# Attention, routing and two MLPs on one core: probabilities times v in one go, and both heads' tails returned to partitions 0 to 63

## The chip, the cores and the metric

One NeuronCore of a Trainium2 chip runs the whole program. The metric is the device time of one execution in microseconds (us), lower being better. The kernel before took 1168.46 us as the median of three runs (1166.98 to 1168.68).

## The reference, cut to what matters

```
# q, k, v: (4, 12, 448, 64) float32; g_q, g_k: (64,)
rmsnorm(x, g) = x / sqrt(mean(x*x, -1) + 1e-6) * g
scores = 1/8 * rmsnorm(q, g_q) @ rmsnorm(k, g_k).T      # per batch and head, 448 x 448
attn   = exp(scores - rowmax) ; attn /= sum(attn) + 1e-9
x      = (attn @ v) gathered to 1792 tokens x 768
logits = x @ w_gate + modality_bias[modality_id]          # 8 experts
e      = argmax(logits); gate = softmax(logits)[e]
y      = gate * (relu(x @ w1[e]) @ w2[e])                 # each token by its one expert
out    = g(y @ w_in) @ w_out                              # g: 0, (h+1)^2/4 or h by range
```

## The kernel before, in words

The program has an attention stage (to about 346 us of the profile), then the experts, then a dense MLP. Attention works on 24 pairs of heads (six pairs per batch element). A pair has seven row tiles of scores: a head has 448 rows, three full tiles of 128 for each head (tiles 0 to 2 and 4 to 6), and one tile (3) for the 64 last rows, the tail, of both heads together.

The loop of lines 453 to 466 walks over slots n = 7p + u, with p the pair and u the tile. In a slot TensorE transposes the probabilities of five slots ago (`turn_p`, L284) and makes the scores of this slot (`scores`, L264). ScalarE takes the exponentials (`expo`, L275). VectorE and ScalarE share the copies of the transposed probabilities (`take_p`, L304 and L306). VectorE takes the row maxima (`row_max`, L269). All else hangs on the table `sched`, filled by `put(z + off, f, p)` with z = 7p: functions in a slot are issued in the order in which they were put, and each engine takes its instructions in that order. Below, "slot z+9" means nine slots after the pair's first. The table `place` gives some early pairs other slots.

What touches the change:

- `mix` (L308) multiplies probabilities and v into the tile `av`, one PSUM bank with one buffer: parts 0 and 1 in slot z+11, parts 2 and 3 in slot z+13. L316 has 128 rows of the array and 64 columns (one head), L320 has 64 by 64 (the tail). `mixed` (L325) copies `av` to SBUF on ScalarE in slot z+13.
- `back` (L334), slot z+15, turns the result back by a matmul with `comb`, which holds an identity and the router's weights: three matmuls for full rows (L341), two of 64 by 64 for the tails (L343), which leave one head's tail on partitions 0 to 63 and the other's on 64 to 127, all in one tile `xo`.
- `invert` (L327), slot z+13: the reciprocal of the sums; an addition (L330, GpSimd from the fourth pair on) and a reciprocal on VectorE (L332).
- `finish_pair` (L1536), slot z+15: three VectorE operations scale `xo` into `x`, `lg` and `xt` (L1542, L1544, L1545). After a batch element's last pair it also sends `x` and `xt` to DRAM and calls `bias_into`.
- `Route.columns` (L603) is a generator that the loop advances one step at a time by `tick`: a step that yields `True` ahead of a TensorE step waits for the next slot with u = 0. Its first TensorE step is the fold (L619), which brings the second head's tail logits to the lower partitions.
- In PSUM the tag `tq` has two buffers. A pair's slots use it in this order: `xo` (z+15), and for the pairs ahead `turn_k` part 0, `turn_q` part 1, `turn_k` part 1, `turn_q` part 0. For a pair p+2, `turn_k` part 0 (L234), `k_low` part 0 (L241, VectorE, the reader that frees it) and `turn_k` part 1 fall in slots z+9, z+10 and z+11 of pair p. In slot z+11 the table holds `mix` parts 0 and 1 ahead of that `turn_k` part 1.
- For pair p+3, `q_low` (L208, GpSimd) is put in slot z+9 of pair p, after the functions of pair p, and `turn_q` part 0 (L217) in slot z+12.

After the loop the last pair's rest is written out by hand (lines 469 to 475), and `on_route` (L1209) advances the routing between the experts' matmuls; `SKIP` names the points at which it makes no TensorE step.

Of the kernel before, what the change touches and what calls it, by code (L numbers as in the profile page):

```python
# [16 lines left out]
E = 8  # L17
# [6 lines left out]
WARM = 40  # L24
TICKS = 2
NPAIRS = 24
SKIP = (3, 4, 7)
KT = SLOTS // 128
NT = E * KT

# [1 line left out]
def attention(tc, ctx, q, k, v, const, ps, late, finish_pair, tick, early):  # L32
# [7 lines left out]
    nc = tc.nc  # L40
    B, H, S, D = q.shape
# [285 lines left out]
    def invert(p):  # L327
        R = st[p]
        d = sm_p.tile([128, 7], F32, name="d", tag="d", bufs=3)
        (nc.vector if p < 3 else nc.gpsimd).tensor_scalar(out=d, in0=R["sum"], scalar1=1.0, scalar2=1e-9, op0=ALU.mult, op1=ALU.add)  # L330
        R["r"] = sm_p.tile([128, 7], F32, name="r", tag="r", bufs=3)
        nc.vector.reciprocal(out=R["r"], in_=d)  # L332

    def back(p):  # L334

        R = st[p]
        r = p % (H // 2)
        t = ps.tile([128, 7, 72], F32, name="xo", tag="tq")
        o = R["o"]
        for c in range(3):  # L340
            nc.tensor.matmul(out=t[:, 2 * c:2 * c + 2], lhsT=o[:, 128 * c:128 * c + 128], rhs=comb[:, r], start=True, stop=True)  # L341
        for i, h in enumerate(halves2):
            nc.tensor.matmul(out=t[h, 6], lhsT=o[h, 384:S], rhs=comb[h, r, i], start=True, stop=True)  # L343
        R["xo"] = t

    def finish(p):
        R = st[p]
        finish_pair(*divmod(p, H // 2), R["xo"], R["r"])
        st[p] = None


# [12 lines left out]
    def put(n, f, p, *a):  # L364
        m = place.get(p, {}).get(f.__name__, n)
        sched.setdefault(m if type(m) is int else m[a[0]], []).append((f, (p,) + a))
# [12 lines left out]
            put(z + off, f, bt[0])  # L379
    for p in range(NP):  # L380
        z = 7 * p
        put(z + 11, mix, p, (0, 1))
        put(z + 13, mix, p, (2, 3))
        for off, f in ((-16, scale_k), (-15, scale_q), (-13, q_high), (-12, q_low), (13, invert), (13, mixed), (15, back), (15, finish)):
# [93 lines left out]
class Route:  # L478
# [7 lines left out]
    def __init__(self, tc, const, cp, tmp, ps, ps_tag, ident):  # L486
        nc = tc.nc
        self.nc, self.tc, self.ps, self.ps_tag = nc, tc, ps, ps_tag
        self.cp, self.tmp, self.ident = cp, tmp, ident
        C = lambda shape, name, dt=F32: cp.tile(shape, dt, name=name)  # L490

        def iota(t, pattern, base, mult):
            nc.gpsimd.iota(t, pattern=pattern, base=base, channel_multiplier=mult, allow_small_or_imprecise_dtypes=True)
            return t
        self.cold = iota(C([128, NDEST], "cold"), [[1, NDEST]], 0, 0)
        self.pcol = iota(C([128, 1], "pcol"), [[0, 1]], 0, 1)
        self.d14 = iota(C([128, E], "d14"), [[-KT, E]], 0, 1)
# [8 lines left out]
        self.fold = C([128, 64], "fold")  # L506
# [12 lines left out]
        self.lg = C([128, 16, E], "lgs")  # L519
        nc.gpsimd.memset(self.lg, 0.0)  # L520
        self.tok, self.gat = C([128, 128], "tok", F32R)[0:NT], C([128, 128], "gat")[0:NT]
        self.base = C([128, 5, E], "base")
        self.gate = C([128, 16], "gate")
        self.midx = const.tile([128, NDEST], I32, name="midx")
        self.pidx = const.tile([128, NDEST], I32, name="pidx")
        self.gslot = const.tile([128, NDEST], F32, name="gslot")
        self.first = const.tile([1, 1], I32, name="first")
        self.ctl = const.tile([1, 2, NDEST], I32, name="ctl")

    def copies(self):  # L530
# [3 lines left out]
        for p in (slice(0, 64), slice(64, 128)):  # L534
            nc.scalar.activation(out=self.fold[p], in_=self.ident[p, p], func=ACTF.Copy)

    def load(self, modality_id, modality_bias):
        nc, mid = self.nc, self.mid
# [56 lines left out]
    def bias_into(self, dst, b):  # L595

        nc = self.nc
        nc.vector.memset(dst, 0.0)
        bm = self.bm[:, 4 * b:4 * b + 4]
        nc.vector.tensor_copy(out=dst[:, 0:6].rearrange("p (c i) e -> p c i e", i=2)[:, :, 0], in_=bm[:, 0:3])  # L600
        nc.vector.tensor_copy(out=dst[0:64, 6], in_=bm[0:64, 3])

    def columns(self, b, parts):  # L603

# [10 lines left out]
        ls = T([128, 7, E], "ls")  # L615
# [6 lines left out]
        lv = ls[:, 0:6].rearrange("p (c i) e -> p c i e", i=2)  # L622
        tt(out=lb[:, 0:3], in0=lv[:, :, 0], in1=lv[:, :, 1], op=ALU.add)
# [852 lines left out]
def tile_kernel(ctx: ExitStack, tc: tile.TileContext, q, k, v, g_q, g_k, moe_modality_id, moe_w_gate, moe_modality_bias,  # L1476
                moe_w1, moe_w2, moe2_w_in, moe2_w_out, out):
    nc = tc.nc
    with tc.manual_schedule():
# [8 lines left out]
        with ExitStack() as c0:  # L1488
# [44 lines left out]
            X = {}  # L1533
            steps, last_wait = [], [0]

            def finish_pair(b, r, xo, rc):  # L1536
                if r == 0:
                    X[b] = (xp.tile([128, 3, 12, 64], F32, name="x", tag="x"), xp.tile([128, 6, 64], F32, name="xt", tag="xt"),
                            rt.tile([128, 7, 7, E], F32, name="lg", tag="lg"))
                x, xt, lg = X[b]  # L1540
                rb = rc.rearrange("p (u o) -> p u o", o=1)
                nc.vector.tensor_tensor(out=x[:, :, 2 * r:2 * r + 2], in0=xo[:, 0:6, 0:64].rearrange("p (c i) d -> p c i d", i=2),  # L1542
                                        in1=rb[:, 0:6].rearrange("p (c i) o -> p c i o", i=2).to_broadcast([128, 3, 2, 64]), op=ALU.mult)
                nc.vector.tensor_tensor(out=lg[:, :, r], in0=xo[:, :, 64:72], in1=rb.to_broadcast([128, 7, E]), op=ALU.mult)  # L1544
                nc.vector.tensor_scalar(out=xt[:, r], in0=xo[:, 6, 0:64], scalar1=rc[:, 6:7], scalar2=None, op0=ALU.mult)  # L1545
                if r == 5:
                    t0 = 448 * b
                    nc.sync.dma_start(out=xt_d[t0:t0 + 384].rearrange("(p c) d -> p c d", c=3), in_=x.rearrange("p c h d -> p c (h d)"))
                    tv = xt_d[t0 + 384:t0 + 448].rearrange("p (r i d) -> p i r d", i=2, d=64)
                    for i in range(2):  # L1550
                        nc.sync.dma_start(out=tv[:, i], in_=xt[64 * i:64 * i + 64])
                    route.bias_into(lg[:, :, 6], b)
                    steps.append([route.columns(b, lg), False])

            moe.m.ps, moe.m.turn_tag = ps, "tq"
# [52 lines left out]
```

## Time and profile before

| | |
|---|---|
| median of the runs | 1168.46 us |
| profiled execution | 1169.01 us, its span 1167.3 us |
| TensorE (PE) busy | 1135.8 us, 97% of the span |
| VectorE (DVE) busy | 826.2 us, 71% |
| ScalarE (ACT) busy | 677.4 us, 58% |
| GpSimd (POOL) busy | 369.2 us, 32% |
| mean granted TensorE clock | 0.989 |

The profile's times are from the start of the span. Matmuls are pipelined: the printed durations overlap, so the cost of a group is read from its start to the start of the next. A float32 matmul shows as two records. "Idle before, releaser" is how long an engine stood still ahead of an instruction and what ended that. The profiled execution took 0.55 us longer than the median.

### The profile page before, as it was taken

The page shows a single profiled execution, that of the slowest core. Times are in us where ns is not written, and L with a number is a line of the kernel's source. Part 1 is how long each engine was busy: PE and PEld are TensorE (multiplying, and loading weights), DVE is VectorE, ACT ScalarE, POOL GpSimd, SP SyncE. Part 2 cuts the span into 40 slices and gives each one's busy share as a digit, 9 for nine tenths or more (in the row PEclk, how much of TensorE's full clock was granted, in tenths as well). Part 3 has the DMA queues.
Part 4 walks back from the last instruction along what each step waited for, and adds up shares of the span by engine and source line. Part 5 has one row for each costly group of instructions (what it writes and reads, how often), then busy time and mean ns, then how long its engine had stood idle before and what let it go on. Part 6 is the DMA issues. An engine that isn't in the chain of part 4 may idle for free. (4 is left out here: it accounts for less than half of the span.)

```text
span 1167.3 us, 20022 instructions
## 1 busy us (share of the span) xinstructions
PE 1135.8 (97%) x7093; PEld 957.5 (82%) x7093; DVE 826.2 (71%) x1551; ACT 677.4 (58%) x1374; POOL 369.2 (32%) x571
## 2 busy tenths in 40 slices
PE   6999999999999999999999999999999999999997
PEld 5667777777768998999999978888888888888996
DVE  6776877877757667888989978884644446444674
ACT  5778777777643566665555645544534345433664
POOL 4666565645220203255544434440200010000100
PEclk8999999999998999999999999999999999999999
DMA  4323324322227689899999723340200001000100
GB/s 105 80 72 87 112 64 117 82 57 80 59 67 245 194 285 295 276 324 289 286 291 310 250 88 99 106 132 4 109 1 1 1 28 55 1 1 1 56 1 28
DMA packets 144593, 138.17 MB, mean 118 GB/s; under 512 B 39134, under 2 KB 125150, under 8 KB 143972
## 3 DMA queue, kind: packets, MB, share of 16 engines
q1 hardware_dynamic: 139822, 120.04, 33.8%
q0 software_dynamic: 4000, 16.53, 4.0%
q8 instruction: 58, 0.95, 0.3%
q14 instruction: 51, 0.42, 0.1%
q10 hardware_dynamic: 662, 0.23, 0.1%
HBM read 117.23 MB, written 18.10 MB: 116 GB/s over the span
## 5 line engine op out<-in xcount | busy, mean ns | idle before, releaser
L934 DVE TENSOR_TENSOR l<-ld,h 128x768 fp32r<-128x768 f32 x159 | 151.5, 970 | 18.4 <-ACT h L929 15.5
L906 POOL TENSOR_SCALAR cva<-cva 128x384 f32<-128x384 f32 x64 | 110.2, 1724 | 144.0 <-ACT cva L905 143.8
L929 ACT ACTIVATE h<-ld 128x768 fp32r<-128x768 f32 x159 | 130.5, 840 | 10.1 <-PE hs L953 6.5
L1426 POOL DMA_INDIRECT out_dram<-ld,oidx x11 | 13.0, 1182 | 336.1 <-ACT ld L1423 212.4
L275 ACT ACTIVATE P<-s,nb 128x448 f32<-128x448 f32 x144 | 91.3, 634 | 34.1 <-DVE nb L269 29.9
L269 DVE TENSOR_REDUCE nb<-s 128x1 f32<-128x448 f32 x168 | 102.6, 614 | 10.7 <-PE s L264 10.1
L1378 ACT ACTIVATE u<-hp,half 128x512 f32<-128x512 f32 (+1 forms) x64 | 40.4, 631 | 108.5 <-PE hp L942 108.5
L1385 DVE SCALAR_TENSOR_TENSOR w<-u 128x512 f32<-128x512 f32 (+1 forms) x64 | 39.9, 623 | 85.3 <-ACT u L1378 85.2
L306 DVE COPY pT<-pt 128x448 f32<-128x448 f32 x96 | 59.6, 621 | 55.6 <-PE pt L284 55.4
L942 PE MATMUL hp<-yh,h 128*128 128x512 f32 (+1 forms) x384 | 89.0, 368 | 2.3 <-PEq L1329 2.3
L976 PE MATMUL a<-l,gh 128*128 128x512 f32 x240 | 89.8, 403 | 0.0
L976 PE MATMUL a<-h,gh 128*128 128x512 f32 x240 | 89.0, 400 | 0.0
L976 PE MATMUL a<-h,gl 128*128 128x512 f32 x240 | 88.8, 399 | 0.0
L1150 ACT ACTIVATE rh<-hp 128x256 fp32r<-128x256 f32 x64 | 24.6, 384 | 109.2 <-PE hp L942 106.8
L942 PE MATMUL hp<-yl,h 128*128 128x512 f32 (+1 forms) x384 | 87.5, 364 | 0.0
L942 PE MATMUL hp<-yh,l 128*128 128x512 f32 (+1 forms) x384 | 87.2, 363 | 0.0
L1393 DVE TENSOR_TENSOR gl<-u,gh 128x512 fp32r<-128x512 f32 (+1 forms) x64 | 40.3, 629 | 64.2 <-ACT gh L1392 64.1
L284 PE MATMUL pt<-ident,P 128*128 128x128 f32 x504 | 83.9, 275 | 0.1
L1392 ACT ACTIVATE gh<-u 128x512 fp32r<-128x512 f32 (+1 forms) x64 | 36.9, 576 | 81.2 <-PE a L977 78.6
L942 PEld LDWEIGHTS hp<-yl,h 128*128 128x128 f32 x384 | 67.1, 190 | 11.4
L942 PEld LDWEIGHTS hp<-yh,h 128*128 128x128 f32 x384 | 64.6, 191 | 14.0 <-PEq L1329 2.6
L942 PEld LDWEIGHTS hp<-yh,l 128*128 128x128 f32 x384 | 66.7, 189 | 11.2
(331 smaller groups left out, 3200.9 us busy)
## 6 DMA issues: line engine op xcount, KB each, us to landing
ld<-in_moe_w_dram SPq DMA_DIRECT2D x160, 384.0 KB
raw<-in_moe_w_in_dram SPq DMA_DIRECT2D x32, 384.0 KB
ld<-in_moe_w_out_dram SPq DMA_DIRECT2D x26, 384.0 KB
rawk<-in_k_dram SPq DMA_DIRECT2D x24, 192.0 KB
rawv<-in_v_dram SPq DMA_DIRECT2D x24, 192.0 KB
xt_d<-x SPq DMA_DIRECT2D x4, 1152.0 KB
kn<-kn SPq DMA_DIRECT2D x20, 224.0 KB
rawq<-in_q_dram SPq DMA_DIRECT2D x23, 192.0 KB
```

The source lines that it names most:

```text
L269: nc.vector.tensor_reduce(out=R["nb"][:, u:u + 1], in_=R["s", u], op=ALU.max, axis=AX.X, negate=True)
L275: nc.scalar.activation(out=o, in_=R.pop(("s", u)), func=ACTF.Exp, bias=R["nb"][:, u:u + 1], accum_out=R["sum"][:, w:w + 1])
L284: nc.tensor.transpose(out=out, in_=src, identity=ident)
L306: nc.vector.tensor_copy(out=R["PT", m], in_=t)
L906: nc.gpsimd.tensor_scalar(out=R["a"], in0=R["a"], scalar1=2.0 ** -15, scalar2=122879.9921875, op0=ALU.max, op1=ALU.min)
L929: nc.scalar.activation(out=h, in_=src, func=ACTF.Copy)
L934: (engine or self.nc.vector).tensor_tensor(out=l, in0=src, in1=h.bitcast(F32), op=ALU.subtract)
L942: nc.tensor.matmul(out=t[:, 0:n], lhsT=w[:, k], rhs=x[:, k, 0:n], start=i == 0 and k == 0, stop=i == 2 and k == 5)
L976: nc.tensor.matmul(out=a[j], lhsT=p[:, c], rhs=q[:, 0:512], start=first and i == 0, stop=last and i == 2)
L1378: nc.scalar.activation(out=u, in_=t[:, s], func=ACTF.Relu, scale=0.5, bias=half)
L1385: nc.vector.scalar_tensor_tensor(out=w, in0=u, scalar=1.0, in1=u, op0=ALU.min, op1=ALU.mult)
L1393: nc.vector.tensor_tensor(out=gl[:, 0:n], in0=u, in1=gh[:, 0:n].bitcast(F32), op=ALU.subtract)
```

## The change

- `mix` of a pair runs whole in slot z+13.
- `back` makes one matmul for both tails, with 64 output partitions and 144 columns, into a tile `xs` that shares the one buffer of `av`; `xo` keeps the full rows alone.
- `invert` moves to slot z+9 and issues a DMA from the GpSimd queue: the tail sums of the second head, 64 values on partitions 64 to 127, to partitions 0 to 63 (tile `rt`).
- `finish_pair` makes six VectorE operations: `x`, `lg` of full rows, and `xt` and `lg` for each head's tail. The tails' logits lie side by side, so `lg` has eight columns of tiles and the fold with its matmul, its PSUM tile and its two set-up copies on ScalarE goes; the second head's part is added by VectorE. `bias_into` (now two memsets and two copies) runs after the fifth pair of a batch element and not after the sixth. `xt` goes to DRAM by one DMA and not two.
- `SKIP` gets the point 0.

```
-SKIP = (3, 4, 7)
+SKIP = (0, 3, 4, 7)
...
     def invert(p):
...
         nc.vector.reciprocal(out=R["r"], in_=d)
+        R["rt"] = sm_p.tile([64, 1], F32, name="rt", tag="rt", bufs=3)
+        nc.gpsimd.dma_start(out=R["rt"], in_=R["r"][64:128, 6:7])
...
     def back(p):
...
-        for i, h in enumerate(halves2):
-            nc.tensor.matmul(out=t[h, 6], lhsT=o[h, 384:S], rhs=comb[h, r, i], start=True, stop=True)
-        R["xo"] = t
+        t2 = ps.tile([64, 2, 72], F32, name="xs", tag="av", bufs=1)
+        nc.tensor.matmul(out=t2, lhsT=R["o"][:, 384:S], rhs=comb[:, r], start=True, stop=True)
+        R["xo"] = t[:, 0:432].rearrange("p (u d) -> p u d", u=6), t2
...
-        put(z + 11, mix, p, (0, 1))
-        put(z + 13, mix, p, (2, 3))
-        for off, f in (..., (13, invert), (13, mixed), (15, back), (15, finish)):
+        put(z + 13, mix, p, (0, 1, 2, 3))
+        for off, f in (..., (9, invert), (13, mixed), (15, back), (15, finish)):
...
     def bias_into(self, dst, b):
-        nc.vector.memset(dst, 0.0)
+        nc.vector.memset(dst[:, :, 6], 0.0)
+        nc.vector.memset(dst[64:128, 6:8, 0:6], 0.0)
...
     def columns(self, b, parts):
...
         nc.vector.tensor_reduce(out=ls, in_=parts.rearrange("p u r e -> p u e r"), op=ALU.add, axis=AX.X)
-        yield True
-        pf = self.ps.tile([64, E], F32, name="pf", tag=self.ps_tag)
-        nc.tensor.matmul(out=pf, lhsT=self.fold, rhs=ls[:, 6], start=True, stop=True)
         yield False
...
-        nc.vector.tensor_copy(out=lb[0:64, 3], in_=pf)
+        tt(out=lb[0:64, 3], in0=ls[0:64, 6], in1=ls[0:64, 7], op=ALU.add)
...
-            def finish_pair(b, r, xo, rc):
+            def finish_pair(b, r, xo, xs, rc, rt_):
...
+                if r == 4:
+                    route.bias_into(lg, b)
...
-                nc.vector.tensor_tensor(out=lg[:, :, r], in0=xo[:, :, 64:72], in1=rb.to_broadcast([128, 7, E]), op=ALU.mult)
-                nc.vector.tensor_scalar(out=xt[:, r], in0=xo[:, 6, 0:64], scalar1=rc[:, 6:7], scalar2=None, op0=ALU.mult)
+                nc.vector.tensor_tensor(out=lg[:, 0:6, r], in0=xo[:, :, 64:72], in1=rb[:, 0:6].to_broadcast([128, 6, E]), op=ALU.mult)
+                for i, s in enumerate((rc[0:64, 6:7], rt_)):
+                    nc.vector.tensor_scalar(out=xt[:, r, i], in0=xs[:, i, 0:64], scalar1=s, scalar2=None, op0=ALU.mult)
+                    nc.vector.tensor_scalar(out=lg[0:64, 6 + i, r], in0=xs[:, i, 64:72], scalar1=s, scalar2=None, op0=ALU.mult)
```

## Rows read from the trace of the kernel before

**Rows 1.** Busy time by engine of two stretches: each engine's busy us, then clock, DMA share, GB/s

```profile
60.00:336.00 276.00, 272.51 (x1855) 196.26 (x1855) 211.05 (x533) 203.93 (x548) 148.28 (x330) 0.99 0.30 84
336.00:362.00 26.00, 21.32 (x134) 16.31 (x133) 16.69 (x62) 8.98 (x16) 3.38 (x4) 0.87 0.42 130
```

**Rows 2.** Timeline of PE in one pair: start, us, instruction, records, idle before

```profile
212.12 0.37 PE L264 MATMUL s<-kl,Q 128*128 128x448 f32 x1
212.42 1.72 PE L316 MATMUL av<-pT,rawv 128*64 128x448 f32 x8
214.07 0.55 PE L234 MATMUL tk<-ident,kn 128*128 128x128 f32 x3
...
216.56 0.97 PE L316 MATMUL av<-pT,rawv 128*64 128x448 f32 x4
217.47 0.98 PE L320 MATMUL av<-pT,rawv 64*64 64x384 f32 x6
218.37 0.33 PE L284 MATMUL pt<-ident,pm 128*128 128x128 f32 x1
...
220.56 0.37 PE L264 MATMUL s<-kl,Q 128*128 128x448 f32 x1
220.76 0.90 PE L341 MATMUL xo<-comb,osb 128*128 128x144 f32 x6
221.59 0.34 PE L343 MATMUL xo<-comb,osb 64*64 64x72 f32 x4
221.86 0.33 PE L284 MATMUL pt<-ident,pm 128*128 128x128 f32 x1
```

**Rows 3.** Timeline of PE around a fold

```profile
206.03 0.37 PE L264 MATMUL s<-kl,Q 128*128 128x448 f32 x1
206.33 0.28 PE L619 MATMUL pf<-ls,fold 128*64 128x8 f32 x2
206.54 0.44 PE L284 MATMUL pt<-ident,pm 128*128 128x128 f32 x2
```

**Rows 4.** Timeline of the start, DVE and PE

```profile
27.06 0.74 DVE L241 SCALAR_TENSOR_TENSOR kl<-tk,gg,kh 128x512 fp32r<-128x512 f32 x1
27.86 0.55 PE L234 MATMUL tk<-ident,kn 128*128 128x128 f32 x3 [0.63 <-DVE kl L241]
```

**Rows 5.** Timeline of DVE in a pair with no routing step, and PE's `mix` beside it

```profile
248.68 0.56 DVE L1542 TENSOR_TENSOR x<-xo,r 128x384 f32<-128x384 f32 x1 [0.39 <-PE xo L343]
249.16 0.20 DVE L1544 TENSOR_TENSOR lg<-xo,r 128x56 f32<-128x56 f32 x1
249.28 0.28 DVE L1545 TENSOR_SCALAR xt<-xo,r 128x64 f32<-128x64 f32 x1
249.47 0.61 DVE L306 COPY pT<-pt 128x448 f32<-128x448 f32 x1
...
251.36 0.62 DVE L269 TENSOR_REDUCE nb<-s 128x1 f32<-128x448 f32 x1 [0.74 <-PE s L264]
251.90 0.74 DVE L241 SCALAR_TENSOR_TENSOR kl<-tk,gg,kh 128x512 fp32r<-128x512 f32 x1
252.33 0.60 PE L316 MATMUL av<-pT,rawv 128*64 128x448 f32 x2
```

**Rows 6.** Timeline of DVE and PE in a pair with routing steps

```profile
146.62 0.60 PE L316 MATMUL av<-pT,rawv 128*64 128x448 f32 x2
146.84 0.74 DVE L241 SCALAR_TENSOR_TENSOR kl<-tk,gg,kh 128x512 fp32r<-128x512 f32 x1
```

**Rows 7.** The operations on tile `lg`: count, ns min/median/max

```profile
L601 DVE COPY lg<-bm x4: 678/679/2200, 117.2 to 347.5; 64x8 f32<-64x8 f32 x4
```

**Rows 8.** Timeline of POOL and PE in slot z+10 of the fourth pair

```profile
77.25 1.13 POOL L208 TENSOR_TENSOR qs<-qn,qs 128x448 fp32r<-128x448 f32 x1 [1.76 <-ACT qs L203]
...
78.44 0.54 PE L217 MATMUL tq<-identr,qs 128*128 128x128 f32 x4 [2.11 <-DVE yi L124]
```

**Rows 9.** Timeline of POOL: a DMA that it issues

```profile
370.24 1.04 POOL L1049 DMA_INDIRECT xg<-xt_d,midx  x1 [0.31 <-issue]
```

**Rows 10.** Timeline of PE at the end of attention

```profile
347.49 0.63 PE L987 MATMUL tp<-ident,xg 128*128 128x128 f32 x4 [1.06 <-DVE lg L598]
...
353.54 0.26 PE L669 MATMUL pr<-oh,tri_r 128*128 128x40 f32 x1 [1.92 <-DVE oh L641]
```

More of the change, by code (lines that the diff above doesn't have):

```diff
@@ L337, in back @@
         r = p % (H // 2)
-        t = ps.tile([128, 7, 72], F32, name="xo", tag="tq")
-        o = R["o"]
+        t = ps.tile([128, 512], F32, name="xo", tag="tq")
         for c in range(3):
-            nc.tensor.matmul(out=t[:, 2 * c:2 * c + 2], lhsT=o[:, 128 * c:128 * c + 128], rhs=comb[:, r], start=True, stop=True)
-        for i, h in enumerate(halves2):
-            nc.tensor.matmul(out=t[h, 6], lhsT=o[h, 384:S], rhs=comb[h, r, i], start=True, stop=True)
-        R["xo"] = t
+            nc.tensor.matmul(out=t[:, 144 * c:144 * c + 144], lhsT=R["o"][:, 128 * c:128 * c + 128], rhs=comb[:, r], start=True, stop=True)
+        t2 = ps.tile([64, 2, 72], F32, name="xs", tag="av", bufs=1)
+        nc.tensor.matmul(out=t2, lhsT=R["o"][:, 384:S], rhs=comb[:, r], start=True, stop=True)
+        R["xo"] = t[:, 0:432].rearrange("p (u d) -> p u d", u=6), t2
     def finish(p):
         R = st[p]
-        finish_pair(*divmod(p, H // 2), R["xo"], R["r"])
+        finish_pair(*divmod(p, H // 2), *R["xo"], R["r"], R["rt"])
         st[p] = None
@@ L381, in attention @@
         z = 7 * p
-        put(z + 11, mix, p, (0, 1))
-        put(z + 13, mix, p, (2, 3))
-        for off, f in ((-16, scale_k), (-15, scale_q), (-13, q_high), (-12, q_low), (13, invert), (13, mixed), (15, back), (15, finish)):
+        put(z + 13, mix, p, (0, 1, 2, 3))
+        for off, f in ((-16, scale_k), (-15, scale_q), (-13, q_high), (-12, q_low), (9, invert), (13, mixed), (15, back), (15, finish)):
             put(z + off, f, p)
@@ L505, in __init__ @@
         self.tri_r, self.ones_r = C([128, 128], "tri_r", F32R), C([128, 128], "ones_r", F32R)
-        self.fold = C([128, 64], "fold")
         self.bias = C([128, 2, E], "bias")
@@ L533, in copies @@
         nc.scalar.activation(out=self.ones_r, in_=self.ones, func=ACTF.Copy)
-        for p in (slice(0, 64), slice(64, 128)):
-            nc.scalar.activation(out=self.fold[p], in_=self.ident[p, p], func=ACTF.Copy)
     def load(self, modality_id, modality_bias):
@@ L597, in bias_into @@
         nc = self.nc
-        nc.vector.memset(dst, 0.0)
+        nc.vector.memset(dst[:, :, 6], 0.0)
+        nc.vector.memset(dst[64:128, 6:8, 0:6], 0.0)
+        v = dst[:, :, 6].rearrange("p (c i) e -> p c i e", i=2)
         bm = self.bm[:, 4 * b:4 * b + 4]
-        nc.vector.tensor_copy(out=dst[:, 0:6].rearrange("p (c i) e -> p c i e", i=2)[:, :, 0], in_=bm[:, 0:3])
-        nc.vector.tensor_copy(out=dst[0:64, 6], in_=bm[0:64, 3])
+        nc.vector.tensor_copy(out=v[:, 0:3, 0], in_=bm[:, 0:3])
+        nc.vector.tensor_copy(out=v[0:64, 3, 0], in_=bm[0:64, 3])
     def columns(self, b, parts):
@@ L614, in columns @@
         tt, ts = nc.vector.tensor_tensor, nc.vector.tensor_scalar
-        ls = T([128, 7, E], "ls")
+        ls = T([128, 8, E], "ls")
         nc.vector.tensor_reduce(out=ls, in_=parts.rearrange("p u r e -> p u e r"), op=ALU.add, axis=AX.X)
-        yield True
-        pf = self.ps.tile([64, E], F32, name="pf", tag=self.ps_tag)
-        nc.tensor.matmul(out=pf, lhsT=self.fold, rhs=ls[:, 6], start=True, stop=True)
         yield False
         lb = self.lg[:, c0:c1]
-        lv = ls[:, 0:6].rearrange("p (c i) e -> p c i e", i=2)
-        tt(out=lb[:, 0:3], in0=lv[:, :, 0], in1=lv[:, :, 1], op=ALU.add)
-        nc.vector.tensor_copy(out=lb[0:64, 3], in_=pf)
+        lv = ls.rearrange("p (c i) e -> p c i e", i=2)
+        tt(out=lb[:, 0:3], in0=lv[:, 0:3, 0], in1=lv[:, 0:3, 1], op=ALU.add)
+        tt(out=lb[0:64, 3], in0=ls[0:64, 6], in1=ls[0:64, 7], op=ALU.add)
         yield False
@@ L1534, in tile_kernel @@
             steps, last_wait = [], [0]
-            def finish_pair(b, r, xo, rc):
+            def finish_pair(b, r, xo, xs, rc, rt_):
                 if r == 0:
-                    X[b] = (xp.tile([128, 3, 12, 64], F32, name="x", tag="x"), xp.tile([128, 6, 64], F32, name="xt", tag="xt"),
-                            rt.tile([128, 7, 7, E], F32, name="lg", tag="lg"))
+                    X[b] = (xp.tile([128, 3, 12, 64], F32, name="x", tag="x"), xp.tile([64, 6, 2, 64], F32, name="xt", tag="xt"),
+                            rt.tile([128, 8, 7, E], F32, name="lg", tag="lg"))
                 x, xt, lg = X[b]
+                if r == 4:
+                    route.bias_into(lg, b)
                 rb = rc.rearrange("p (u o) -> p u o", o=1)
-                nc.vector.tensor_tensor(out=x[:, :, 2 * r:2 * r + 2], in0=xo[:, 0:6, 0:64].rearrange("p (c i) d -> p c i d", i=2),
+                nc.vector.tensor_tensor(out=x[:, :, 2 * r:2 * r + 2], in0=xo[:, :, 0:64].rearrange("p (c i) d -> p c i d", i=2),
                                         in1=rb[:, 0:6].rearrange("p (c i) o -> p c i o", i=2).to_broadcast([128, 3, 2, 64]), op=ALU.mult)
-                nc.vector.tensor_tensor(out=lg[:, :, r], in0=xo[:, :, 64:72], in1=rb.to_broadcast([128, 7, E]), op=ALU.mult)
-                nc.vector.tensor_scalar(out=xt[:, r], in0=xo[:, 6, 0:64], scalar1=rc[:, 6:7], scalar2=None, op0=ALU.mult)
+                nc.vector.tensor_tensor(out=lg[:, 0:6, r], in0=xo[:, :, 64:72], in1=rb[:, 0:6].to_broadcast([128, 6, E]), op=ALU.mult)
+                for i, s in enumerate((rc[0:64, 6:7], rt_)):
+                    nc.vector.tensor_scalar(out=xt[:, r, i], in0=xs[:, i, 0:64], scalar1=s, scalar2=None, op0=ALU.mult)
+                    nc.vector.tensor_scalar(out=lg[0:64, 6 + i, r], in0=xs[:, i, 64:72], scalar1=s, scalar2=None, op0=ALU.mult)
                 if r == 5:
@@ L1548, in finish_pair @@
                     nc.sync.dma_start(out=xt_d[t0:t0 + 384].rearrange("(p c) d -> p c d", c=3), in_=x.rearrange("p c h d -> p c (h d)"))
[L1549 to L1552, printed above, removed]
+                    nc.sync.dma_start(out=xt_d[t0 + 384:t0 + 448], in_=xt.rearrange("p r i d -> p (r i d)"))
                     steps.append([route.columns(b, lg), False])
```

## The prediction, made before the change was run

> **What bounds the kernel now.** I read the busy time by stretch first, then the waits of TensorE, then the timelines engine by engine. In the 276 us from 60 to 336, TensorE is busy 272.5 us at a granted clock of 0.99 (the 2.4 GHz level), while VectorE has 211 us and ScalarE 204 us of work [rows 1]. So TensorE's queue sets the pace of attention, and its matmuls follow each other almost without a gap. The other engines' waits inside a pair cost nothing today. What the change can win there is TensorE time, and what it can lose is a new place where TensorE waits. After 362 the experts and the MLP run on the same full TensorE, so what attention gains or loses stays in the end time. The second stretch, 336 to 362, is different: TensorE is busy 21.3 of 26 us and the clock 0.87 [rows 1]. There its waits are for VectorE, and two are named: 1.06 us ahead of a transposition and 1.92 us ahead of the routing's count [rows 10].
>
> **Matmuls that are removed or merged.** I cost each by starts.
>
> A 448-column score matmul ahead of an ordinary group takes 0.20 us (220.56 to 220.76); ahead of a group of 64 output columns it takes 0.30 (212.12 to 212.42) [rows 2]. So entering the 64-column form costs 0.10 us. The Trainium skill, "TensorEngine Tiling (Array Packing)", section "Key Properties", says that a change of tiling mode drains the engine; these two rows agree with it. Four av matmuls, eight records, take 1.65 us to the next group, two of them 0.91 [rows 2]. One in the middle is therefore (1.65 - 0.91)/2 = 0.37, and each group carries 0.17 at its two ends. Before, a pair pays (0.10 + 1.65) + (0.10 + 0.91) = 2.76. In one go it pays 0.10 + 0.91 + 4 x 0.37 = 2.49. That saves 0.27 us in each of 23 pairs (the last is written out by hand and stays split): **-6.2 us**.
>
> The two tail matmuls of `back` take 0.27 us for four records (221.59 to 221.86) [rows 2]. The new one has two records of 64 weights and 144 columns. Its nearest row is the fold, with the same weights and 8 columns: 0.21 [rows 3]. From below it is 0.21. From above it is the 0.27 that it replaces: an `xo` record of 144 columns with twice the weights costs 0.83/6 = 0.14, the step into the tail's form included. I take 0.22, near the fold: **-1.2 us** over 24 pairs (0 to -1.4). The same section of the Trainium skill speaks against this edit: different tiles of the array can run in parallel, so the two heads' tails would already share their time. Were the two halves counted at half their 0.27 us, the new matmul would cost 2 us more over 24 pairs and not 1.2 less; the timeline shows 0.27 spent, so the sum keeps that.
>
> The fold costs 0.10 to enter and 0.21 to run [rows 3]; three of four stand in the full stretch: **-0.9 us**. Its set-up copies on ScalarE stand where ScalarE does not hold TensorE up: 0.
>
> **The wait that takes the place of `mix`.** In slot z+11 the first half of `mix` stood ahead of `turn_k` part 1. That transposition writes the PSUM buffer of `turn_k` part 0, which `k_low` must first read on VectorE. The dependency can be seen bare at the start, where no `mix` stands between: `k_low` ends at 27.06 + 0.74 = 27.80 and TensorE, 0.63 us idle, goes on at 27.86 [rows 4]. In a pair without routing steps VectorE is idle for 0.74 us until the scores of tile 3 are there, then takes the maximum and `k_low`, which ends at 251.90 + 0.74 = 252.64; the first half of `mix` began at 252.33 [rows 5]. Without it TensorE would want the transposition at 252.33 - 0.10 = 252.23. It finds the buffer taken for 0.41 us, and 0.06 more for the handover as at the start: 0.47. This floor comes from TensorE's own scores and does not go away when VectorE is faster. In sixteen pairs (the seventh to the twenty-second) the same comparison gives 0.41 to 1.06 us; the rows show the smallest and the largest, where `k_low` ends at 147.58 and TensorE would come at 146.52 [rows 5, 6]. At the floor: 16 x 0.47 = 7.5 us. In four of the first six pairs some 0.4 remains (in three of them another transposition stands between), 1.6; the fifth and the last pairs have none. Together **+9.1 us**. Queued behind that transposition are the next scores and all that hangs on them. Later in the slots the one long `mix` gives ScalarE and VectorE 1.5 us more to catch up, so I see no second stall from it.
>
> **What makes VectorE later than the floor.** `finish_pair` takes 0.12 us from `lg` to `xt` and 0.19 from `xt` to the next [rows 5]; three more such operations are about +0.4, the reciprocal of `invert` now ahead of `k_low` +0.1. Against that, `x` no longer waits for the tails (it stood 0.39 idle until TensorE ended them [rows 5]): -0.3. Pairs at the floor swallow this in their 0.74 us of idle. Pairs that are late already (eleven of the sixteen) do not. `bias_into`, with a copy of 0.68 us [rows 7], moves to the fifth pair of each batch element and makes one more pair late, by some 0.4; the routing steps start earlier because they no longer wait for the fold's slot. I take 0.2 to 0.4 us in nine pairs, **+3 us**; bounds 0 (all swallowed) and +6 (the lateness of today kept in full).
>
> **The new DMA on GpSimd's queue.** It waits there for VectorE's reciprocal, then takes GpSimd's issue time. The nearest row is an indirect DMA, 1.04 us [rows 9]. Behind it stands `q_low` of pair p+3, which TensorE needs three slots later. In the plain pair the copy that starts at 249.47 [rows 5], a maximum and the reciprocal end at about 250.75, the issue at 251.8 and `q_low`, 1.13 us [rows 8], at 253. TensorE leaves the stall at 252.70 and asks for it after that transposition and one slot's transpositions and scores, 1.2 us later, at 253.9. So it is hidden with 0.9 us to spare, and the cover is gone once the issue takes some 2 us. One place has no cover: in slot z+9 of the fourth pair stands `q_low` of the seventh, and TensorE wants it one slot later and waits 2.11 us already [rows 8]. There reciprocal and issue come on top: **+2.4 us** (0 to 2.7). The DMA's landing has six slots, some 10 us, and is hidden.
>
> **The end of attention.** `bias_into` is gone from it, three small operations come, and the routing's first steps run through to the count without the fold. VectorE reaches the count's input about 1.5 us earlier, and TensorE waits 1.92 for it [rows 10]: **-1.5 us**. Bounds: 0, and -3.0 (both waits gone) with 3.4 us more if the clock stays at 2.4 GHz there (0.13 short of full over 26 us [rows 1]).
>
> **Sum.** -6.2 - 1.2 - 0.9 + 9.1 + 3 + 2.4 - 1.5 = +4.7 us on the profiled 1169.0, or 1173.7; that execution is 0.55 over the median, so against the runs it is **1173 us**, slower by 0.4%. Two runs of this kernel can be told apart by about 0.2%, 2.3 us.
>
> **Rivals.**
> 1. The floor alone, with a good end: no lateness above it, the place in the fourth pair half absorbed, the end's waits and clock won back in part. 9.1 - 8.3 + 1.2 - 4 = -2, or 1166, with the ends at 1163 and 1170. For it: the late pairs' excess is small beside the 0.74 us of VectorE's idle time. Against it: those late pairs have no such idle time.
> 2. The other side: the stall at `turn_k` part 1 does not come, because VectorE has freed the buffer in time. Then -8.3, -1.5 and about nothing lost: 1159 us. It decides where `k_low` ends ahead of 252.23 in the plain pair; break-even lies at a stall of about 0.3 us for each pair. Against it stand the order of the table and the wait at the start [rows 4].
> 3. The DMA's issue takes 2 us or more. `q_low` then comes after `turn_q` wants it in some sixteen pairs: at 3 us 1.1 us each, 17 us, 1190; at 2.5 us 1182. For it: GpSimd's issue is known here only from another kind of DMA [rows 9], and VectorE is busy three quarters of the time. The Trainium skill, "SBUF — State Buffer", section "SBUF: two separate sides", says that GpSimd cannot write descriptors while VectorE copies from SBUF to SBUF in a fast mode, and gives 3.1 us for a DMA that takes 0.62 alone; no row here shows it.
> 4. Gains and the stall cancel: VectorE's lateness and the fourth pair's stall come to nothing, the end gains 1.5. 1168 us, no change.
>
> **Chances.** The sum as it stands 0.48 (0.42 of it above 1170.8, 0.06 within 0.2%), rival 1 0.27 (0.15 faster, 0.12 same), rival 2 0.08, rival 3 0.09, rival 4 0.08. So faster 0.23, same 0.26, slower 0.51. The forecast's own range is 1170 to 1178. To leave out no more than rivals 2 and 3 the range is 1163 to 1181; its low end is all gains with the best end (-8.3 + 9.1 - 6.4 = -5.6), its high end the upper bounds of every loss (+9.5) and some of rival 3.
>
> **What would show it.** In the profile after, TensorE should list a wait of `tk` for `kl` L241 some 20 times, 0.4 to 1 us each, 9 to 12 us in all, and one of `tq` in the fourth pair of over 4 us. A pair's `mix` should be one group of 3.3 us, the tail matmul 0.22 us, GpSimd's new issue about 1 us. The waits ahead of the count should shrink by about 1.5 us. The prediction is wrong if that wait for `kl` is missing or far under 0.4 us, if `tq` waits for `q_low` in most pairs, or if the clock of the stretch falls because of the new gaps.

## The result, and the profile after

The changed kernel takes 1184.31 us (median of four runs, 1182.92 to 1186.28), the kernel before 1168.57 beside it: ratio 1.0146, 95% interval 1.0119 to 1.0172. It is slower by 15.7 us. I had forecast 1173 with a range to 1181: the direction was right, the size was not. The profiled execution took 1182.92 us, its span is 1181.2.

Busy time by engine of two stretches of the kernel after; columns as in [rows 1], whose second stretch begins 17 us earlier:

```profile
60.00:336.00 276.00, 259.74 (x1721) 189.63 (x1718) 208.96 (x577) 199.09 (x531) 155.73 (x348) 0.99 0.28 76
353.00:379.00 26.00, 21.63 (x145) 16.25 (x145) 19.09 (x72) 10.79 (x19) 3.97 (x5) 1.00 0.42 138
```

In the first stretch TensorE now stands 16.3 of 276 us where it stood 3.5. VectorE and ScalarE are no busier than in [rows 1], so nothing is overloaded: TensorE waits. In the second stretch the granted clock is 1.00 and not 0.87.

What TensorE waited for up to 380 us, kernel after (us in all, times, longest):

```profile
PE tq L217 <- POOL qs L208: 6.5, 2, 4.6
PE tk L234 <- DVE kl L241: 5.8, 12, 0.7
...
PE tk L234 <- ACT Q L219: 3.5, 4, 1.1
PE pt L284 <- ACT pm L275: 2.8, 6, 0.9
PE pr L665 <- DVE oh L637: 2.2, 1, 2.2
...
PE tp L983 <- DVE lg L1542: 0.5, 1, 0.5
```

The expected wait of `tk` for `kl` is there. So are two that I had not forecast: `tk` waits for `Q`, ScalarE's copy of `turn_q`'s result, and `pt`, the first transposition of slot u = 5, for `pm`, the exponentials of tile 3. TensorE's timeline of one pair, kernel after:

```profile
250.26 0.45 PE L264 MATMUL s<-kh,Q 128*128 128x448 f32 x1
250.54 0.36 PE L264 MATMUL s<-kl,Q 128*128 128x448 f32 x1
251.56 0.52 PE L234 MATMUL tk<-ident,kn 128*128 128x128 f32 x3 [0.66 <-DVE kl L241]
252.40 0.33 PE L284 MATMUL pt<-ident,pm 128*128 128x128 f32 x1 [0.32 <-ACT pm L275]
...
254.55 2.48 PE L316 MATMUL av<-pT,rawv 128*64 128x448 f32 x12
256.96 0.98 PE L320 MATMUL av<-pT,rawv 64*64 64x384 f32 x6
257.86 0.33 PE L284 MATMUL pt<-ident,pm 128*128 128x128 f32 x1
...
260.60 0.90 PE L342 MATMUL xo<-comb,osb 128*128 128x144 f32 x6
261.43 0.46 PE L344 MATMUL xs<-comb,osb 128*64 128x144 f32 x2
261.82 0.33 PE L284 MATMUL pt<-ident,pm 128*128 128x128 f32 x1
```

Read by starts, as in [rows 2]: `mix` whole takes 2.41 + 0.90 = 3.31 us, as worked out. A score matmul before `tk` should cost 0.20; here it is 1.02 to `tk` and 0.84 from there to `pt`, where [rows 2] show the `mix` half and then no wait. The table's idle time (0.66 and 0.32) is less than the loss by starts, because the ends of matmuls are modelled. The tail matmul takes 0.39, more than the 0.27 that it replaces.

### The profile page after: what moved, and what is told of

Read it like the earlier page. It is cut to its first block, busy times and chain, and to the rows that moved or that the text cites. A ratio compares the mean times of both kernels' runs of the same rounds, so it can differ in the third digit from the quotient of the medians.

```text
span 1181.2 us, 20031 instructions
## 1 busy us (share of the span) xinstructions
PE 1131.9 (96%) x7037; PEld 954.6 (81%) x7037; DVE 832.9 (71%) x1627; ACT 678.8 (57%) x1372; POOL 380.3 (32%) x595
## 5 line engine op out<-in xcount | busy, mean ns | idle before, releaser
L1422 POOL DMA_INDIRECT out_dram<-ld,oidx x11 | 12.7, 1153 | 335.7 <-ACT ld L1419 213.0
```

## The experiments

Each kernel ran in five rounds beside the kernel before, in four groups (the table's first four kernels, then four, three and four; medians of before: 1167.8, 1167.3, 1167.5 and 1166.9). Between the groups the kernel before moves by 0.9 us, and differences across groups are no better than that.

| kernel | median us | ratio to before, 95% |
|---|---|---|
| e1_split | 1171.6 | 1.0034 (1.0018 to 1.0050) |
| e2_merge | 1181.7 | 1.0118 (1.0103 to 1.0133) |
| e3_turnk | 1191.2 | 1.0201 (1.0185 to 1.0218) |
| e5_wide | 1183.6 | 1.0132 (1.0116 to 1.0147) |
| e7_osb | 1184.7 | 1.0141 (1.0116 to 1.0165) |
| e7_klow | 1210.5 | 1.0370 (1.0344 to 1.0395) |
| e8_back | 1184.1 | 1.0138 (1.0114 to 1.0161) |
| e9_split_wide | 1165.7 | 0.9990 (0.9976 to 1.0003) |
| e12_one | 1172.1 | 1.0034 (1.0015 to 1.0053) |
| e10_chain | 1195.6 | 1.0237 (1.0207 to 1.0267) |
| e11_best | 1181.3 | 1.0117 (1.0084 to 1.0150) |
| e13_hole | 1190.0 | 1.0208 (1.0191 to 1.0226) |
| e14_hole_wide | 1185.8 | 1.0166 (1.0148 to 1.0185) |
| e16_hole_wide_place | 1186.0 | 1.0162 (1.0148 to 1.0176) |
| e15_split_place | 1163.4 | 0.9965 (0.9953 to 0.9976) |

### Which part of the change costs

e1_split, on the changed kernel:

```
-        put(z + 13, mix, p, (0, 1, 2, 3))
+        put(z + 11, mix, p, (0, 1))
+        put(z + 13, mix, p, (2, 3))
```

> The changed kernel with mix split again as before (parts 0 and 1 in slot z+11, parts 2 and 3 in z+13); all the rest of the change stays. My theory: the first half of mix covers the time in which k_low still reads the buffer of turn_k, so the waits of tk for kl L241 (5.8 us in 12, and the rest of about 12 us by the starts) go, and with them the new waits of pt for pm (2.8 us); the split costs back 6.2 us. Net -8.6 on 1184.3: about 1176 us. Rival A, the cost lies in the rewritten return (the longer xs matmul, six VectorE operations, the DMA on GpSimd's queue) and the lateness of VectorE that it brings: the waits shrink little, the split costs 6, and the time is 1184 to 1190. Rival B, all of the loss is the merge: the time comes back to 1168.

e2_merge is the opposite edit, on the kernel before.

> The kernel before with one edit alone: mix of a pair whole in slot z+13. My theory: mix saves 6.2 us (0.27 in each of 23 pairs) and the waits of tk for k_low take 10 to 12, with 1 to 3 more behind mix where ScalarE is late: about 1174 us (1172 to 1177), slower than before without any of the rest. The first rival: with VectorE's old work the buffer is free in time in most pairs, and the merge alone gains: 1162 to 1166.

The split gives back 12.7 us; the merge alone costs 13.9. My number for the first was too small (8.6 us), for the second as well (6). All the rest of the change costs 3.8 us (e1_split against its kernel before). TensorE's waits from 60 to 350 us in e1_split:

```profile
PE tq L217 <- POOL qs L208: 4.9, 1, 4.9
PE tp L984 <- DVE lg L1543: 0.5, 1, 0.5
PE pt L284 <- ACT pT L304: 0.2, 1, 0.2
```

No wait for `kl`, none for `pm`. In e2_merge, up to 380 us, both are there, though nothing but the place of `mix` differs from the kernel before:

```profile
PE tk L234 <- DVE kl L241: 8.1, 13, 0.8
...
PE pt L284 <- ACT pm L275: 4.1, 10, 0.6
PE tk L234 <- ACT Q L219: 2.8, 4, 0.9
```

### How much cover is missing, and where

e12_one moves a quarter of `mix`, e13_hole moves it whole into the other slot. On the changed kernel:

```
# e12_one
+        put(z + 11, mix, p, (0,))
+        put(z + 13, mix, p, (1, 2, 3))
# e13_hole; part 3 opens the sum and part 2 closes it
+        put(z + 11, mix, p, (3, 0, 1, 2) if p < NP - 1 else (0, 1, 2, 3))
```

> The changed kernel with only part 0 of mix in slot z+11 and parts 1 to 3 in z+13. A graded test of the theory of cover: the whole merge leaves TensorE waiting between the last scores of tile 3 and the first transposition that needs tile 3, because the path from those scores over the row maximum to k_low and to the exponentials takes 2.2 to 3.1 us there and TensorE has 1.66 us of other work. Part 0 puts 1.01 us back, so that the hole has 2.67 us of work: by the changed kernel's own intervals only seven pairs still wait, 2 us in all. The saving of 6.2 us by the merge is given back in full, since mix is entered twice again. So 1173 to 1175, some 10 us under the changed kernel, with a quarter of mix moved. If two parts are needed (the path stretches with the work in front of it), it stays above 1178.

> The changed kernel with mix whole in slot z+11, and not in z+13, in the order of parts 3, 0, 1, 2, so that part 2, whose last input is copied in that same slot, comes last; nothing else is changed. Theory of cover: it is not the merge that costs but where the merged mix stands. In slot z+11 it fills the time in which tile 3 goes through row maximum, k_low and exponentials, so that the waits of some 19 us go and the saving of 0.27 us in 23 pairs stays: 6.2 us under the kernel with the split alone (1171.6), so 1164 to 1167. Rival: a block of 3.3 us starves ScalarE and VectorE wherever it stands (they get no scores meanwhile), the waits turn up in another slot, and the time stays above 1178.

e12_one came out as worked out, a little better: a quarter of `mix` in slot z+11 is worth 12.2 us. e13_hole refutes my theory, and its rival came true: 1190, so filling that slot is not enough. To see why, I measured two intervals of every pair by starts on TensorE. Interval A runs from the last score matmul of tile 3 (slot u = 3) to the first transposition that needs tile 3 (slot u = 5). Interval B runs from the last score matmul of tile 6 to the scores two slots later, which stand right behind the first transpositions that need tile 6. "Rest" is the sum over the pairs without the part of `mix` that stands inside (with 0.10 for entering its form; 23 pairs in A, 22 in B): 1.75 and 1.91 us a pair where it is split in two, 1.01 and 2.66 in e12_one, 3.41 where it is whole.

| kernel | A | rest of A | B | rest of B |
|---|---|---|---|---|
| before | 90.1 | 49.8 | 87.3 | 45.3 |
| e1_split | 90.4 | 50.1 | 86.6 | 44.6 |
| e12_one | 75.4 | 52.2 | 102.7 | 44.2 |
| after | 68.7 | 68.7 | 119.4 | 44.3 |
| e13_hole | 127.6 | 49.2 | 70.3 | 70.3 |

The rest of A grows by 18.6 us from e1_split to the kernel after, the rest of B by 25.7 to e13_hole. With the merge's 6.2 us these give differences of +12.1 and +18.6 us (A and B together); the runs say +12.7 and +18.4. So each half of the split `mix` stood where TensorE must otherwise wait for a tile to go through its maximum and its exponentials: the first half behind tile 3, the second behind tile 6, and the whole can cover only one of the two. In e12_one the plain pairs' A is 2.64 to 2.69 us, the 1.66 + 1.01 of their work without a wait; pairs that were longer after (2.93, 3.12) kept their length.

Where e13_hole waits from 60 to 350 us, and ScalarE's timeline of one pair there:

```profile
PE pt L284 <- ACT P L275: 13.8, 21, 1.0
PE tq L217 <- POOL qs L208: 3.7, 1, 3.7
PE pt L284 <- ACT pT L304: 3.6, 5, 0.9
```

```profile
227.40 0.65 ACT L275 ACTIVATE pm<-s,nb 128x448 f32<-128x448 f32 x1
...
231.14 0.58 ACT L236 ACTIVATE kh<-tk,gg 128x384 fp32r<-128x384 f32 x1 [3.01 <-PE tk L234]
231.62 0.63 ACT L275 ACTIVATE P<-s,nb 128x448 f32<-128x448 f32 x1
...
234.79 0.67 ACT L275 ACTIVATE P<-s,nb 128x448 f32<-128x448 f32 x1
```

ScalarE stands 3.01 us at `kh`, whose transposition is queued behind the block of `mix`, and the exponentials of the next tile stand behind `kh`. Then TensorE runs through three slots in 3.3 us (by its starts) and waits for the last tile's exponentials. Whether `turn_k` one slot later would mend this variant was not tried.

### Five attempts on a single path in interval A

```
# e3_turnk
-  (-3, turn_k, 1), (-2, k_low, 1)
+  (-2, turn_k, 1), (-1, k_low, 1)
# e7_klow
-  (-4, k_low, 0)
+  (-5, k_low, 0)
# e7_osb (22: dict(mixed=167) in place)
-  (13, mixed)
+  (14, mixed)
# e8_back
-  (15, back), (15, finish)
+  (18, back), (18, finish)
# e10_chain: in slots u = 2, 3 row_max stands ahead of take_p and tick, and
-  (-4, turn_q, 1)
+  (-3, turn_q, 1)
```

> The changed kernel with turn_k part 1 and k_low part 1 one slot later (z+12 and z+13 of the pair two before), where k_low part 0 has had a whole slot more; the pairs with a place of their own keep it. My theory: the waits of tk for kl L241 go (12 us by the starts; 5.8 us in the table of waits), mix stays whole, and about 1172 us comes out. If the delay only moves the wait (turn_q part 0, which also wants a buffer of this tag in slot z+12, or the scores that need kh and kl), the time stays at 1182 to 1186.

1191.2: it was a miss. The wait moved to the second path (TensorE's waits up to 380 us, kernel e3_turnk):

```profile
PE pt L284 <- ACT pm L275: 20.2, 20, 1.7
```

`k_low` and the exponentials both start from the scores of tile 3 and take about the same time. With the buffer out of the way A's rest is 65.9 and not 68.7, and the moved transpositions are now work outside the hole.

> The changed kernel with k_low part 0 one slot earlier on VectorE (z+9 in place of z+10), ahead of the row maximum of tile 3 and not behind it, so that the buffer of turn_k part 0 is free some 0.7 us earlier. Theory A (the loop through ScalarE): the wait of tk for kl goes, but TensorE waits as long one step later, at the transposition that needs the exponentials of tile 3: 1181 to 1186 us, and the table of waits shows pt for pm L275 in its place. Theory B (the buffer is the bound, as predicted): the 12 us of that wait go and the time falls to 1172 to 1176.

Theory B falls: the buffer is not the one bound, and the wait moves to `pt` as theory A said. In ten of the sixteen pairs from the 7th to the 22nd A stays as it was (1.97 to 2.94 us; 2.18 to 2.93 in the kernel after). But theory A's 1181 to 1186 missed too, by 25 us: in the other six A lasted 3.9 to 6.3 us. In these a short routing step stands ahead of the maximum of tile 3 on VectorE, now behind `k_low` and so later. It lasts 3.18 us (`eq`, three pairs) or 1.54 (`lf`, three pairs) where the kernel after shows 0.19 and 0.12: it begins while GpSimd issues `invert`'s DMA and ends as the GpSimd operations behind that DMA end. So these 25 us are no price of a path. TensorE's waits up to 380 us, then VectorE's and GpSimd's timelines of one of the six pairs:

```profile
PE pt L284 <- ACT pm L275: 27.5, 21, 4.1
```

```profile
129.76 3.18 DVE L626 TENSOR_TENSOR eq<-lgs,mxl 128x32 f32<-128x32 f32 x1
132.86 0.61 DVE L269 TENSOR_REDUCE nb<-s 128x1 f32<-128x448 f32 x1
...
129.31 0.58 POOL L334 DMA_DIRECT2D rt<-r  x1 [3.17 <-DVE r L332]
...
131.94 0.94 POOL L198 TENSOR_TENSOR qn<-rawq,rq 128x448 f32<-128x448 f32 x1
```

> The changed kernel with mixed (the copy of av to SBUF on ScalarE) one slot later, in z+14 (the pair before the last keeps its slot). Theory A, a loop through ScalarE: in the changed kernel ScalarE stands up to 2.4 us at that copy until the whole mix has ended (34.1 us in 20 pairs), then works off copy and exponentials almost without a pause up to those of tile 3, for which TensorE's first transposition of slot z+12 waits. One slot later the exponentials of slot z+14 run during mix, and the chain behind mix gets shorter by one of 0.62 us: the waits at tk and pt shrink in some 18 pairs, -6 to -11 us, 1173 to 1178 us. Theory B, the buffer that k_low frees is the bound: VectorE, and not ScalarE, sets it, and the time stays at 1182 to 1186.

Theory A falls here. ScalarE's wait at the copy halves, from the first row (kernel after, 60 to 350) to the second (e7_osb), and the time stays:

```profile
ACT osb L325 <- PE av L320: 34.1, 20, 2.4
```

```profile
ACT osb L325 <- PE av L320: 16.9, 16, 2.2
```

> The changed kernel with back and finish of a pair three slots later (z+18 in place of z+15), so that the 1.22 us of xo and xs stand in the slot that mix parts 0 and 1 have left, ahead of turn_k part 1. Theory: what is missing there is work for TensorE of any kind while the exponentials of tile 3 are made; xo then stands in the hole and no longer in a full slot, and the waits between the scores of tile 3 and the first transposition behind them (some 19 us in all) shrink by up to 1.2 us in each pair: 1166 to 1174 us. Against it: xo then takes the buffer of turn_k part 0 itself and waits for kl in place of tk; if that wait is the bound and not the exponentials, the time stays at 1182 or above.

It stayed at 1184. The work stands in the hole, but behind the wait: `xo` takes the buffer that `k_low` must free, and `xs`, `tk` and `pt` come after it (TensorE's waits up to 380 us):

```profile
PE xo L342 <- DVE kl L241: 5.0, 13, 0.4
```

> The changed kernel, mix whole, with the path through tile 3 made shorter: in slots u = 2 and 3 the row maximum stands ahead of the copy of transposed probabilities and the routing step on VectorE, and turn_q part 1 is one slot later (z+11), so that its copy on ScalarE stands behind the exponentials of tile 3. Theory: where a pair waits over 0.5 us, VectorE has come late to the maximum of tile 2 (six operations of finish_pair, a routing step and a copy stand ahead of it), the exponentials of tile 2 start late, and copies stand ahead of those of tile 3 on ScalarE. Then the intervals of 2.6 to 3.1 us fall to about 2.2: 4 to 8 us, 1176 to 1180. If they stay, the order on VectorE is not what makes these pairs late, and the time stays at 1182 to 1186.

Half of this held: in five pairs interval A shrank by 0.4 to 0.5 us (among them 2.93 to 2.45, 2.80 to 2.30 and 2.60 to 2.19). In six others, the six of e7_klow, it grew by 1.1 to 1.5 us, and the time by 11. In three of these a routing step of 32 columns now stands ahead of `k_low` and takes 1.54 us, in the other three one of 128 columns takes 1.35 to 1.37 where 0.35 is usual; all six begin during the issue of `invert`'s DMA. VectorE's timeline of one:

```profile
211.35 1.54 DVE L630 TENSOR_TENSOR eq<-lgs,mxl 128x32 f32<-128x32 f32 x1
212.81 0.74 DVE L241 SCALAR_TENSOR_TENSOR kl<-tk,gg,kh 128x512 fp32r<-128x512 f32 x1
```

What makes the late pairs late, VectorE's queue or ScalarE's, these runs do not settle: e10_chain moved work on both. With `mix` whole no attempt on a single path paid, and two lost much more to VectorE's long routing steps; one quarter of `mix` as cover is enough.

### The return: the tail matmul and `invert`

e5_wide, and e9_split_wide with the split besides:

```
-        t2 = ps.tile([64, 2, 72], F32, name="xs", tag="av", bufs=1)
-        nc.tensor.matmul(out=t2, lhsT=R["o"][:, 384:S], rhs=comb[:, r], start=True, stop=True)
+        t2 = ps.tile([128, 2, 72], F32, name="xs", tag="av", bufs=1)
+        nc.tensor.matmul(out=t2, lhsT=R["o"][:, 384:512], rhs=comb[:, r], start=True, stop=True)
```

> The changed kernel with the tail matmul 128 weights wide: its SBUF input is 512 columns wide with 64 zeros behind the tail, and the upper 64 output partitions are not read, so that TensorE stays in the form of the three matmuls ahead of it. My theory: the 0.39 us from xs to the next group is a matmul of the 64-column form that is entered alone for two records; in the wide form it takes 0.25 to 0.28 and the score or transposition behind it keeps its time: -0.11 to -0.2 us in each of 24 pairs, 1180 to 1182 us. Rival: the 0.39 us is the time of 144 columns at float32 whatever the form, and the time stays at 1184.

> The changed kernel with mix split as before and with the wide tail matmul (128 weights, the upper half zeros and not read). In the merged kernel the wide tail saved 0.29 us of TensorE time in each pair (xs 0.25 in place of 0.39, xo and the transposition behind it without a change of form) and the waits grew by as much, so that the time stayed. Where mix is split TensorE has no such waits, and the theory says that the saving counts in full: 24 x 0.29 = 7 us under the split kernel's 1171.6, 1164 to 1166. The rival: the time of this part is hidden there too, and it stays at 1171.

The lines above are cut: both runs also keep `osb` in two fixed tiles of 512 columns, the last 64 zero. TensorE in e9_split_wide:

```profile
246.10 0.90 PE L345 MATMUL xo<-comb,osb 128*128 128x144 f32 x6
246.84 0.41 PE L347 MATMUL xs<-comb,osb 128*128 128x144 f32 x2
247.08 0.27 PE L287 MATMUL pt<-ident,pm 128*128 128x128 f32 x1
247.19 0.49 PE L287 MATMUL pt<-ident,P 128*128 128x128 f32 x3
```

`xo` takes 0.74, `xs` 0.24 and the transposition behind it 0.11; in the kernel after 0.83, 0.39 and 0.16. A tail twice as wide is cheaper by 0.29 us a pair. In the merged kernel this gains nothing (1183.6), since A grows by 0.3 in most pairs: the pair's length is set by the path through the tiles. In the split kernel, where TensorE is the bound, it gains 5.9 us of the 7 expected.

e11_best has `invert` in z+10 for all pairs; e15_split_place only for the first and the fourth (slots 10 and 31); e14_hole_wide and e16_hole_wide_place are e13_hole with the wide tail, and with those two places as well.

> Mix split as before, the wide tail matmul, and invert in slot z+10 and not z+9, so that the reciprocal and the DMA on GpSimd's queue stand behind q_low in the pairs with a place of their own. The split kernel with the wide tail took 1165.7. Theory: the waits of turn_q for q_low at the start and in the fourth pair (1.9 and over 4 us, with 2.1 before the change) lose what the DMA added, 2 to 4 us: 1162 to 1164, faster than the kernel before. If GpSimd is late there for another reason, 1165 to 1166.

> Mix split as before and the wide tail (1165.7), with invert of the first and of the fourth pair alone one slot later. Expected: 2 us less, 1163 to 1165; none if the wait for q_low there has another cause.

> As the run before, with the wide tail matmul (128 weights, the upper half zeros and not read). With the split mix the wide tail was worth 5.9 us (1171.6 to 1165.7). If nothing waits in the hole, both savings add: 1158 to 1161, faster than the kernel before by 0.5 to 0.8%. If the pitch is bound by another engine there, the wide tail gains nothing, as in the merged kernel.

> As the run before, with invert of the first and of the fourth pair alone put one slot later (slots 10 and 31), where GpSimd's q_low, for which TensorE waits at once, then stands ahead of the addition, the reciprocal's wait and the DMA of invert. In the kernel with invert at z+10 in all pairs these two places gave back 2 us by the starts, while VectorE's reciprocal stood 24.9 us for GpSimd's addition in the others. Expected: 2 us under the run before, 1156 to 1159. If the wait for q_low has another cause, no difference.

e11_best lost 15.6 us. VectorE's reciprocal in one of its pairs:

```profile
193.06 0.20 DVE L335 RECIPROCAL r<-d 128x7 f32<-128x7 f32 x1 [2.54 <-POOL d L333]
193.17 0.70 DVE L244 SCALAR_TENSOR_TENSOR kl<-tk,gg,kh 128x512 fp32r<-128x512 f32 x1
```

One slot later GpSimd's addition `d` stands behind a run of small steps of another pair, VectorE waits for it (24.9 us in 12 pairs) and `k_low` is next in its queue. So slot z+10 is too late for many pairs. With the first and the fourth alone, e15_split_place takes 1163.4 us, 2.3 less than e9_split_wide, and is faster than the kernel before by 0.35% (0.24 to 0.47). On the block in slot z+11 the expected 1158 to 1161 and 1156 to 1159 fell with e13_hole, and neither edit paid in full: e14_hole_wide gains 4.2 us over e13_hole, the two places nothing more.

## Why the prediction was wrong

The sum was +4.7. The runs split 16.5 us (1184.3 against the 1167.8 of e1_split's group; 15.7 against the kernel before beside it) into -6.2 for `mix`, 18.9 of waits (12.7 + 6.2) and 3.8 for the rest.

**`mix` merged, -6.2: right.** 3.31 us a pair as worked out.

**The waits, 9.1 + 3 = 12.1: the place and the kind right, the size and half of the causes wrong.** This is the step that failed first. I took one cause, that `turn_k` part 1 must wait until `k_low` frees its buffer, for all pairs. By starts, against e1_split without its part of `mix`, the 18.6 us of A are 6.8 ahead of `tk` in eleven pairs that do wait for `k_low`, 5.1 ahead of `tk` in eight pairs that do not, 5.5 at `pt`, and 1.2 in the second and fifth pairs, where TensorE waits for `q_low`.

The floor held where the buffer is `k_low`'s: in the pair of [rows 5] A is 2.19 us against 1.66 of work, 0.53 lost ahead of `tk` where I had 0.47. In the eight other pairs it is not the buffer of `turn_k` part 0 that `turn_k` part 1 gets. In five of them `tk` begins before `k_low` has ended, just behind ScalarE's copy `Q` of `turn_q` part 1; in the other three both end together and the profile names `Q` (1.06 to 1.08 us each, the longest pairs). The pair of [rows 6], in the kernel after, is one of the five: `k_low` ends at 154.80, `Q` at 154.61. My comparison had given 1.06 us for it, the most of all; 0.28 came at `tk` and 0.23 at `pt`. Why the buffer is another one there no run shows.

```profile
154.06 0.74 DVE L241 SCALAR_TENSOR_TENSOR kl<-tk,gg,kh 128x512 fp32r<-128x512 f32 x1
...
154.12 0.49 ACT L219 ACTIVATE Q<-tq 128x384 fp32r<-128x384 f32 x1
...
154.67 0.55 PE L234 MATMUL tk<-ident,kn 128*128 128x128 f32 x3
```

The 5.5 us are the second path: the exponentials of tile 3 come out of the same scores at about the same time, and the transposition of slot u = 5 waits for them behind `tk`. "Later in the slots the one long `mix` gives ScalarE and VectorE 1.5 us more to catch up, so I see no second stall from it" was false: the second stall stands directly behind the first. And seven of the sixteen pairs lost 0.9 to 1.4 us of A against e1_split, where my sum had 0.47 and 0.2 to 0.4 for lateness.

**The tail matmul, -1.2: mis-sized, about +2.8** (0.39 for 0.27, in 24 pairs). "I take 0.22, near the fold" set 8 columns against 144. `xo` shows 0.74/6 = 0.12 us for each record of 144 columns, so two take 0.24 and 0.15 is left for the form. Four records of 72 columns one after another would come to the same 0.39; they took 0.27, which is 0.15 + 0.12, as if the two heads ran side by side. The rule of the Trainium skill that I had weighed ("TensorEngine Tiling (Array Packing)", "Key Properties": tiles work in parallel) gave +2 us, and the trace agrees with it better than with my choice. My upper bound of no loss was therefore no bound.

**The fold, -0.9**: its two records are gone; no run tells this term apart. **VectorE's work**: e1_split shows that, with `mix` split, six operations of `finish_pair` in place of three make TensorE wait nowhere in the full stretch. There is also a gain that my sum did not have. In the kernel before, TensorE waits in three pairs just behind the copies of `bias_into` (60 to 350 us):

```profile
PE pt L284 <- DVE pT L306: 1.3, 3, 0.4
```

With `bias_into` in another pair this wait is gone from e1_split, and A of these three pairs falls from 4.03 or 4.04 to 3.43.

**GpSimd's DMA: +2.4 in the fourth pair, right, and one place missed.** The issue took 0.58 us, not 1.04. GpSimd's timeline of the fourth pair, kernel after:

```profile
78.32 0.21 POOL L330 TENSOR_SCALAR d<-sum 128x7 f32<-128x7 f32 x1
81.69 0.58 POOL L334 DMA_DIRECT2D rt<-r  x1 [3.16 <-DVE mg L585]
82.30 1.14 POOL L208 TENSOR_TENSOR qs<-qn,qs 128x448 fp32r<-128x448 f32 x1
```

The cost is not the issue but the wait for VectorE in front of it. TensorE waits 4.6 us for that `q_low` where [rows 8] had 2.11, and 1.9 at the start, which I had put at nothing (0.2 in e1_split, where half of `mix` stands ahead of it). Putting the two back earned 2.3 us. Rival 3 falls with the 0.58, rivals 1, 2 and 4 with the waits. All 24 issues took 0.57 to 0.77 us; no run shows the 3.1 us that the Trainium skill ("SBUF — State Buffer", "SBUF: two separate sides") gives for a DMA held up by VectorE.

**The end, -1.5: the wrong reason.** The count's wait did not shrink (2.2 us; 1.92 in [rows 10]), the one ahead of the transposition did (0.5 for 1.06). The last `xo` begins 16.85 us later than before (362.00 for 345.15) and the span ends 13.9 later, so 2.95 us come back behind it, with the clock at 1.00 for 0.87 [rows 1], a gain that I had only as a bound. e1_split, with the same routing and a clock of 0.88 from 336 to 380, has nothing of it. What raised the clock no run shows.

## What to carry to other kernels

Before merging or moving a block on the engine that is the bound, ask what each piece covers where it stands: list the results of other engines that the next instructions wait for, and measure the time from their source to their use without the block. Two paths of equal length from one source must both be shortened; a piece of independent work in between covers both. Read pair by pair what a wait is for: the instruction that frees a buffer need not be the one that the order of the code suggests. Price a matmul by its columns and by the form it forces on its neighbours, not by the row with the same weights.

## What the runs showed of the hardware

A float32 matmul of 128 weights and 144 columns behind others of its form costs 0.24 us, one of 64 weights 0.39, with 0.14 more on its two neighbours (granted clock 0.99). GpSimd issued the 64-element DMA in 0.58 us. VectorE's `eq` of 32 columns, 0.19 us elsewhere in e10_chain, took 1.54: it began at 211.35, while GpSimd issued the DMA, and ended as GpSimd's `q_low` ended (211.69 + 1.14 = 212.83). In e7_klow the same step took 3.18 us, to the end of a run of GpSimd operations (131.94 + 0.94 = 132.88). GpSimd's timeline of e10_chain:

```profile
211.09 0.58 POOL L334 DMA_DIRECT2D rt<-r  x1 [2.76 <-DVE mxl L627]
211.69 1.14 POOL L208 TENSOR_TENSOR qs<-qn,qs 128x448 fp32r<-128x448 f32 x1
```

The Trainium skill, "SBUF — State Buffer", "SBUF: two separate sides", says that a VectorE operation with two SBUF inputs and a GpSimd operation that reads SBUF shut each other out for a whole instruction, whichever starts first going ahead. The end of the two agrees with that. `eq` starts before `q_low` in the record, behind the start of the DMA's issue; that the issue already shuts it out is likely from the runs, but no run tests it.
